# Sparse attention and a mixture of experts on one core: row maxima sent as columns by DMA, and tokens as the stationary operand in one block

## The chip, the cores and the metric

The kernel runs on one core of a Trainium2 chip. The metric is the device time of one execution in microseconds. The engines are named as the profile names them: PE (TensorE), with PEld for its weight loads, DVE (VectorE), ACT (ScalarE), POOL (GpSimd) and SP (SyncE). SPq and ACTq are the queues on which SP and ACT issue DMAs.

## The reference, cut to what matters

There are 8 batches of 8 heads with 576 rows and head width 64. Each row keeps only the scores that reach its 32nd largest one:

```python
scores = scale * np.matmul(q, k.transpose(0, 1, 3, 2))
kth = np.partition(scores, -top_k, axis=-1)[..., -top_k:-top_k + 1]
scores = np.where(scores >= kth, scores, -1000000000.0)
scores = scores - np.max(scores, axis=-1, keepdims=True)
attn = np.exp(scores); attn /= attn.sum(-1, keepdims=True) + 1e-09
x = np.matmul(attn, v)                       # then heads side by side: 4608 tokens x 512
do_compute = x @ w_skip > 0                  # the other tokens are passed on as they are
e_idx = np.argmax(xc @ w_gate, axis=1)       # xc: the tokens of do_compute; 8 experts
y[mask] = gate_w[mask, None] * (np.maximum(xc[mask] @ w1[e], 0.0) @ w2[e])
out[do_compute] = xc + y
```

The widths of an expert are 512, 1024 and 512.

## The kernel before, in words

**Attention** goes over 32 pairs of heads. q and k of a pair are loaded, turned on PE (L543), copied out by ACT (`put`, L548 and L554), split on POOL into a rounded high part and the rest (L568, L571), and brought by SP's DMAs (`copy`, L576) into the operands: `QH` and `KK` (128 partitions: high parts in one half, low parts of k in the other half) and `QL` (64 partitions: the low part of q, and below it two more rows). `KO` is the second operand's partner: the high part of k and, in the rows against those two rows of `QL`, the value -1. So what stands in the two rows of `QL` is subtracted from a query's scores in the same product. While the rows are searched they are zero.

A pair has nine **rows** (tiles of 128 queries by 576 keys; `row`). PE forms the scores in PSUM (`qk`, L659), DVE takes the eight largest of seven chunks (`chunk`, L669) and sorts among them (`cand`, L675 and L677), ACT copies the scores out (`take`, L711) and counts those above the 24th (`above_out`, L691, with a read of the accumulator), POOL sets those to zero (`push_out`, L714), DVE adds a marker and finds the next eight (`fill`, L723; `window`, L733), and ACT writes a penalty for everything below the 32nd (`below_out`, L730).

Then there are nine **units** to a pair (`unit`, `block`): PE forms the transposed scores (L873, with 128 partitions of `QH` and `KK`, and L875, with 66 partitions of `QL` and `KO`, which subtracts the maxima), adds the penalties (L880), and ACT takes the exponential (L905). `values` multiplies with v and forms sums and gate logits.

**The maxima** (`maxes`) are handed over twice in a pair, after rows 4 and 8. POOL rounds the column of five or four maxima into `NM` and puts what the rounding left out beside it (L821, L822), PE turns `NM` (L827), ACT copies the turned rows into `mt` (L831), and SP sends them to the two rows of `QL` by row DMAs (L837): four for the first head and two for the second.

**The order** within attention is made when the program is built. Each step goes to a planner (`Plan`) with an engine, a duration, a due time and the steps it follows; the planner sends the instruction that can start first, and among those that can, it takes the earliest due time. Due times are the row's number plus offsets from two tables of numbers, `K` and `FINE`. On each engine the instructions then run in the order in which they were sent. SP is in order too; a DMA that SP issues also waits for the DMA eight before it on SP's queue, since there are eight completion semaphores. There are three PSUM tiles for rows and units together.

**The experts** follow. Tokens are listed by expert in three blocks of 128 (`route`), gathered by POOL, turned (L1158), and multiplied with w1 (`up`, L1223 to L1225: w1 is stationary, the tokens move; three products for high and low parts) and with w2 (`down`, L1246 to L1248). The first expert's first two blocks are gathered before the last batch is done. Its third block waits for the last batch's routing, and is multiplied apart from the others, with 128 moving columns (`upping`). The weights of later experts are loaded and split two experts ahead (`part_hi` L1115 on ACT, `part_lo` L1118 on DVE).

## Time and profile before

| what | value |
|---|---|
| runs | 1150.28, 1151.07, 1150.89 us; median 1150.89 us |
| the profiled execution | 1151.41 us, its span 1149.4 us |
| busy, PE / DVE / ACT / POOL | 1103.8 / 985.4 / 929.3 / 764.9 us |
| instructions, PE / DVE / ACT / POOL | 13012 / 5226 / 1965 / 1027 |
| share of the DMA engines, queue 1 (SP) | 46.0% |

A busy time is the union of the instructions' spans on an engine. Neighbours on ACT and DVE overlap at their ends, so that a row of the timeline with a duration of 0.76 us can be followed 0.66 us after its start by the next; what an instruction costs is read from start to start of neighbours that wait for nothing.

In the stages: up to about 45 us the first rows fill the pipe, then attention runs evenly to about 830 us, its last pair ends at about 864 us, and from there the experts run to 1134 us; the last scattered rows go out behind that.

### The profile page before, as it was taken

To read this page: it belongs to the slowest core of one execution; us is meant where nothing else is said; L and a number is where in the kernel's file an instruction comes from. 1 tells how busy PE (TensorE), PEld (TensorE's weight loads), DVE (VectorE), ACT (ScalarE), POOL (GpSimd) and SP (SyncE) were. 2 spreads that over 40 slices of the span, in tenths; PEclk is the share of its full clock that TensorE was granted. 3 is DMA by queue.
4 is the path that set the end of the run, shared out by engine and by line. 5 is a ranking of instruction groups with operands and counts; after the bars stand their busy time and mean duration, and the time that the engine had idled before them with its cause. 6 is when DMAs were issued, how large, how long until landed. Compare 5 with 4: busy or idle time off the path is not lost. (4 is left out here: it accounts for less than half of the span.)

```text
span 1149.4 us, 37808 instructions
## 1 busy us (share of the span) xinstructions
PE 1103.8 (96%) x13012; PEld 939.4 (82%) x13012; DVE 985.4 (86%) x5226; ACT 929.3 (81%) x1965; POOL 764.9 (67%) x1027
## 2 busy tenths in 40 slices
PE   4799999999999999999999999999999999999996
PEld 4678888888888888888888878887778988899995
DVE  8899999999999999999999999999966756655541
ACT  4899999999999999999999999999972533444430
POOL 7777888888778888887788999888884121222211
PEclk9999999999999999999999999999999999999998
DMA  6544546565544555565446444654147554455300
GB/s 145 120 102 117 127 118 149 120 150 125 138 116 116 141 132 140 123 138 140 117 115 150 105 114 116 159 135 112 29 127 254 185 172 160 162 168 163 120 19 26
DMA packets 197405, 148.43 MB, mean 129 GB/s; under 512 B 100898, under 2 KB 162850, under 8 KB 197204
## 3 DMA queue, kind: packets, MB, share of 16 engines
q1 hardware_dynamic: 190340, 135.54, 46.0%
q0 software_dynamic: 3840, 9.47, 2.5%
q8 instruction: 105, 1.72, 0.6%
q10 hardware_dynamic: 3024, 0.90, 0.3%
q14 instruction: 96, 0.79, 0.2%
HBM read 68.31 MB, written 25.31 MB: 81 GB/s over the span
## 5 line engine op out<-in xcount | busy, mean ns | idle before, releaser
L714 POOL TENSOR_TENSOR xw<-xc,r 128x576 f32<-128x576 f32 x288 | 370.6, 1287 | 126.2 <-ACT r L691 120.4
L669 DVE MAX8 cand<-r 128x8 f32<-128x82 f32 (+1 forms) x2016 | 384.1, 234 | 3.6 <-PE r L659 1.1
L691 ACT ACTIVATE r<-xc,cl 128x576 bf16<-128x576 f32 x288 | 221.7, 770 | 5.5 <-DVE cl L675 4.4
L730 ACT ACTIVATE PEN<-xc,wn 128x576 bf16<-128x576 f32 x288 | 221.0, 769 | 5.0 <-DVE wn L733 4.8
L733 DVE MAX8 wn<-xw 128x8 f32<-128x585 f32 x288 | 217.1, 754 | 2.6 <-POOL xw L714 2.5
L873 PE MATMUL r<-QH,KK 128*128 128x256 f32 (+1 forms) x640 | 188.2, 321 | 5.0 <-ACT PT L905 2.1
L711 ACT ACTIVATE xc<-r 128x576 f32<-128x576 f32 x288 | 183.8, 639 | 6.0 <-DVE cand L669 2.9
L875 PE MATMUL r<-QL,KK 66*128 66x256 f32 (+1 forms) x640 | 173.3, 298 | 0.0
L659 PE MATMUL r<-KK,QH 128*128 128x288 f32 x640 | 161.5, 342 | 11.5 <-ACT xc L711 7.9
L675 DVE MAX8 cl<-cand 128x8 f32<-128x28 f32 (+2 forms) x864 | 164.5, 192 | 5.2
L905 ACT ACTIVATE PT<-r 128x576 f32<-128x576 f32 x256 | 161.8, 642 | 3.5 <-PE r L880 3.5
L1152 POOL DMA_INDIRECT out_dram<-ot,idx x24 | 24.0, 999 | 200.9 <-DVE ot L1151 155.3
L659 PE MATMUL r<-KK,QL 66*128 66x288 f32 x640 | 135.5, 302 | 0.0
L873 PEld LDWEIGHTS r<-QH,KK 128*128 128x128 f32 x640 | 118.3, 190 | 16.7 <-ACT xc L711 6.4
L880 PE MATMUL r<-nbi,PEN 128*128 128x128 bf16 (+1 forms) x1632 | 131.9, 216 | 0.0
L659 PEld LDWEIGHTS r<-KK,QH 128*128 128x128 f32 x640 | 98.0, 195 | 38.4 <-issue 12.1
L1115 ACT ACTIVATE hi<-raw 128x1024 fp32r<-128x1024 f32 x64 | 67.2, 1055 | 71.6 <-PE py L1248 71.3
L1118 DVE TENSOR_TENSOR lo<-raw,hi 128x1024 fp32r<-128x1024 f32 x60 | 73.3, 1225 | 59.1 <-ACT hi L1115 59.1
L875 PEld LDWEIGHTS r<-QL,KK 66*128 66x128 f32 x640 | 118.9, 191 | 0.0
L659 PEld LDWEIGHTS r<-KK,QL 66*128 66x128 f32 x640 | 104.3, 195 | 0.3 <-issue 0.3
L677 DVE MATCH_REPLACE8 cand<-cl,cand 128x28 f32<-128x28 f32 x576 | 103.0, 179 | 0.0
L880 PEld LDWEIGHTS <-PEN 128*128 128x128 bf16 x1632 | 82.3, 99 | 21.2 <-issue 0.4
(272 smaller groups left out, 2511.0 us busy)
## 6 DMA issues: line engine op xcount, KB each, us to landing
raw<-in_moe_w_dram SPq DMA_DIRECT2D x64, 512.0 KB
KK<-HI SPq DMA_DIRECT2D x62, 288.0 KB
QH<-HI SPq DMA_DIRECT2D x124, 144.0 KB
KK<-LO SPq DMA_DIRECT2D x62, 144.0 KB
QL<-LO SPq DMA_DIRECT2D x62, 144.0 KB
raw<-in_k_dram SPq DMA_DIRECT2D x64, 128.0 KB
V<-in_v_dram SPq DMA_DIRECT2D x32, 256.0 KB
raw<-in_q_dram SPq DMA_DIRECT2D x62, 128.0 KB
```

The lines of the kernel that those rows point to most:

```text
L659: nc.tensor.matmul(R(u, w), t[0:k0, c:c + P], KH[i2][0:k0, HB * hd + u:HB * hd + w], start=(k0 == P and x == 0), stop=(k0 < P and x == len ...
L669: nc.vector.max(C[s][:, c], R(CH[c], CH[c + 1]))
L675: nc.vector.max(L[:, 4 * r:4 * r + 8], c)
L691: nc.scalar.activation(RR[s], R() if i in SG else XC[s], AF.Sign, bias=CL[p][:, i, 23:24], scale=-ODD, accum_out=CN[:, s:s + 1])
L711: nc.scalar.activation(XC[s], R(), AF.Copy)
L714: nc.gpsimd.tensor_tensor(xw()[:, 0:S], XC[s], RR[s], op=OP.mult)
L730: nc.scalar.activation(pen, XC[s], AF.Relu, bias=least, scale=-1.0)
L733: nc.vector.max(WN[p][:, i], XW[s] if out_ else R())
L873: nc.tensor.matmul(t, KH[i2][:, ks], QH[i2][:, qs], start=(y == 0), stop=False)
L875: nc.tensor.matmul(t, KO[i2][:, ks], QL[i2][0:D + 2, qs], start=False, stop=False)
L880: nc.tensor.matmul(rb[:, O + c:O + c + z - a], PEN[p][:, PS * i + REM + c0 - o:PS * i + REM + c0 - o + P], nbi[:, a:z], start=False, stop= ...
L905: return pl.add("ACT", 0.535, due + K["ex"] + FINE["ex"][at], lambda: nc.scalar.activation(dst, st["r"], AF.Exp, scale=scale), x, give=[h])
```

## The change

**Maxima.** `NM` becomes two tiles of nine columns. POOL rounds the maxima into them with one copy, what the rounding left out is dropped, and SP sends each column of 128 maxima (64 for the halves of row 4) straight into its piece of `QL`'s single extra row, element by element: six DMAs for the first head and four for the second. PE's turning (L827), ACT's copy (L831) and POOL's second step (L822) are gone. `KO` and `QL` have 65 rows in use in place of 66.

**The first expert's third block** (`late`). The tokens are the stationary operand and w1's quarters move, with 256 columns to a product. The hidden values come out with the tokens on the partitions; two halves of 512 columns are copied to SBUF by ACT (`SL`), turned back on PE in two groups of four, and then go through the relu as before. The first half's `down` products are sent by the planner.

**The start.** The loads of the first q and k stand ahead of everything, on SP and ACT. The casts into `KK` on DVE write one half and are written as a maximum of the source with itself; the other half comes by two DMAs. The gate table's identities come by one DMA in place of twelve copies on POOL, and its clearing covers 18 columns of 146. Tables and clearings that are not needed first stand later. Unused branches are dropped.

**Offsets.** All of `K` and `FINE` is new, and with them the order on every engine. Some durations that the planner assumes are a little shorter (POOL's products 1.255 in place of 1.31).

```diff
-    nc.gpsimd.memset(NM_.bitcast(F32), 0.0)
+    NM_ = [ap_.tile([P, NR], F32R, name=f"NM{i}") for i in range(2)]
...
-            nc.gpsimd.tensor_copy(nm[:, 0:n], cl)
-            nc.gpsimd.tensor_tensor(nm[:, n:2 * n], cl, nm[:, 0:n], op=OP.subtract)
-            nc.tensor.transpose(pm[:, 0:P], NM_, identR)
-            nc.scalar.activation(mt, h.t[0:2 * n, 0:P], AF.Copy)
-            nc.sync.dma_start(dst[a:a + 1].bitcast(F32), src.bitcast(F32))
+        def send(j, r0, c):
+            n = P if j != NM else REM
+                nc.sync.dma_start(QL[p % NQ][D:D + 1, c:c + n].bitcast(F32), nm[r0:r0 + n, j:j + 1].bitcast(F32))
+        x = pl.add("POOL", 0.2, due + FINE["mx"][m0], lambda: nc.gpsimd.tensor_copy(nm[:, i0:i0 + n], CL[p][:, i0:i0 + n, 0]),
+                   [CAND0[NR * p + i] for i in range(i0, i0 + n)], MAXED.get((p - 2, i0 > 0)))
+        MAXED[p, i0 > 0] = [pl.add("SP", 0.67, due + 0.4, lambda y=y: send(*y), x, lag=2.0) for y in rows]
...
-                        nc.tensor.matmul(t, KO[i2][:, ks], QL[i2][0:D + 2, qs], start=False, stop=False)
+                        nc.tensor.matmul(t, KO[i2][:, ks], QL[i2][0:D + 1, qs], start=False, stop=False)
...
-    done = upping(EARLY * P, TN, D1 + 12, turning(0, NB - 1, PX, D1 + 8, g))
+        def product(i, ph):
+            for c in range(CC):
+                nc.tensor.matmul(o, xh[:, c], h1[:, c], start=(c == 0), stop=False)
+                nc.tensor.matmul(o, xh[:, c], l1[:, c], start=False, stop=False)
+                nc.tensor.matmul(o, xl[:, c], h1[:, c], start=False, stop=(c == CC - 1))
+        def back(g, px):
+            for k in range(FC // 2):
+                nc.tensor.transpose(px[:, k * P:(k + 1) * P], SL[g][:, k * P:(k + 1) * P], identF)
+    done = late(D1 + 12, turning(0, NB - 1, PX, D1 + 8, g))
...
-        ops = [("DVE", 0.7, KK[0][up, :, A], two(kA), None, 0), ("ACT", 0.55, QH[0][up, A], qA, None, 0),
+        ops = [("DVE", 0.7, KH[0][up, A], kA, None, 0), ("ACT", 0.55, QH[0][up, A], qA, None, 0),
...
-                    nc.vector.tensor_copy(dst, src)
+                    nc.vector.tensor_tensor(dst, src, src, op=OP.max)
...
-K = dict(qk=-6.898, cand=-10.286, kt=0.696, push=-15.422, ...)
+K = dict(qk=-3.229, cand=-70.654, kt=-66.095, push=-15.835, ...)
```

Where it moves instructions, three places. First SP's queue, over one handing-over of both heads' maxima in the middle of attention, before (L837 sends maxima, L576 brings operands, L509 and L510 load q and k; the numbers behind the names tell buffers apart):

```order
L837 DMA QL_115<-mt 1x4x128
L837 DMA QL_115<-mt 1x2x64
L837 DMA QL_115<-mt 1x4x128
L837 DMA QL_115<-mt 1x2x64
L576 DMA QL_112<-QL_112 2x1280
L509 DMA raw_117<-in_k_dram 128x4x64 x2
L510 DMA rawr<-in_k_dram 64x2x64
L509 DMA raw_118<-in_q_dram 128x4x64 x2
L510 DMA rawr<-in_q_dram 64x2x64
L837 DMA QL_115<-mt 1x4x128 x2
```

And now, from the first head's maxima on (L749 sends a column, L365 and L366 store results, L567 brings operands):

```order
L749 DMA QL_110<-NM_208 1x128x1 x4
L749 DMA QL_110<-NM_208 1x64x1 x2
L365 DMA xd<-xb 512x1x128
L366 DMA xd<-xb 64x128
L365 DMA out_dram<-xb 512x1x128
L366 DMA out_dram<-xb 64x128
L567 DMA KK_108<-HI 64x2x576
L567 DMA KK_108<-LO 64x576
L567 DMA QH_106<-HI 64x576 x2
L567 DMA QL_107<-LO 64x576
L567 DMA QL_107<-QL_107 1x16x80
```

Five more operand copies follow, and then the second head's four columns. What were six DMAs from `mt` are ten from `NM`; now the results' stores and eleven DMAs for the next operands stand between the two heads' maxima, where the loads stood before.

Next ACT's queue in the middle of attention, before:

```order
L730 ACTIVATE PEN_195<-xc,wn 128x576
L548 ACTIVATE TT<-pa 128x512
L905 ACTIVATE PT_123<-r_148 128x576
L831 ACTIVATE mt<-pt 10x128
L691 ACTIVATE r,CN<-xc,cl 128x576
L711 ACTIVATE xc<-r_147 128x576
```

And now, at about the same place (L695, L539, L812, L674 and L679 are the former L730, L548, L905, L691 and L711):

```order
L695 ACTIVATE PEN_203<-xc,wn 128x576
L812 ACTIVATE PT_130<-r_152 128x576
L674 ACTIVATE r,CN<-xc,cl 128x576
L679 ACTIVATE xc<-r_154 128x576
L887 ACTIVATE os_150<-pa 128x64
L885 ACTIVATE os_150<-pa 128x64
```

The row `mt` is gone from ACT; the others come as often as before, in another sequence.

Last PE's queue where the first expert's third block ends, now (L1181 to L1183 are the products, L1187 turns the hidden values back, L1058 turns the next expert's tokens, L1146 to L1148 are `down`):

```order
L1182 MATMUL ph<-lo_17551,xh_17554 128x256
L1183 MATMUL ph<-hi_17547,xl_17555 128x256
L1187 MATMUL px<-identF,sl_17910 128x128 x4
L1058 MATMUL px<-identF,xg_17887 128x128 x4
L1181 MATMUL ph<-hi_17548,xh_17554 128x256
```

Behind the fourth quarter's twelve products there are three `down` products, and then the second group of four turns. Before, eight groups of twelve products with 128 columns stood here, then all 24 `down` products of the block.

More of the change, by code (lines that the diff above doesn't have):

```diff
@@ L80, in tile_kernel, with load_raw @@
     ps_a = att.enter_context(tc.tile_pool(name="ps_a", bufs=1, space=PSUM))
+    RAW = [sp_.tile([P, NM, 2, D], F32, name=f"raw{i}") for i in range(2)]
+    RAWR = sp_.tile([P, 2, D], F32, name="rawr")
+    def load_raw(p, nm, queue):
+        b, hp = divmod(p, H // 2)
+        src = (k, q)[nm]
+        for hh in range(2):
+            queue.dma_start(RAW[nm][:, 0:NM, hh], src[b, 2 * hp + hh, 0:MAIN].rearrange("(p t) d -> p t d", p=P))
+        queue.dma_start(RAWR[nm * REM:(nm + 1) * REM], src[b, 2 * hp:2 * hp + 2, MAIN:S].rearrange("h p d -> p h d"))
+    load_raw(0, 0, nc.sync)
+    load_raw(0, 1, nc.scalar)
     identF = cp.tile([P, P], F32, name="identF")
@@ L276, in tile_kernel @@
     pl = Plan()
-    pl.at.update(ACT=3.0, DVE=6.0, POOL=12.0, SP=0.35)
+    pl.at.update(ACT=4.4, DVE=6.0, POOL=10.5, SP=0.35)
     BT = Res([lambda dt: ps_t.tile([P, 512], dt, name="pt"), lambda dt: ps_a.tile([P, 512], dt, name="pa")])
@@ L503, in load @@
     def load(p):
[L504 to L516 removed]
+        for nm in range(2):
+            if p:
+                LOADED[nm, p] = pl.add("SP", 2.0, max(NR * p - K["ld"], 0 if p == 1 else -99) + 0.5 * nm,
+                                       lambda nm=nm: load_raw(p, nm, nc.sync), TURNED.get((nm, p - 1)), lag=1.5)
+            else:
+                LOADED[nm, p] = pl.add("SP", 0.5, -99 + nm, None, lag=4.2)
     def load_v(p):
@@ L595, in prep @@
         if old:
-            COPIED[p].append(pl.add("SP", 0.67, NR * p - 3, lambda: copy(QL[i][D:D + 2], QL[i][D + 2:D + 4]), old, lag=2.0))
+            COPIED[p].append(pl.add("SP", 0.67, NR * p - 3, lambda: copy(QL[i][D:D + 1], QL[i][D + 1:D + 2]), old, lag=2.0))
     CFREE = {}
@@ L642, in row @@
         PEN[p] = PEN_[p % 2]
-        out_ = i in OUT
-        h = Hold(RW, 1 if out_ and i not in SG else 2)
+        h = Hold(RW, 1)
         R = lambda u=0, w=S: h.t[:, LO_ + u:LO_ + w]
@@ new lines, in row @@
+        rr = A("ACT", 0.765, s + D_["kt"] + J("kt"), above_out, x, tx, PUSHD.get(s - 3), lag=-0.06)
+        fx = A("DVE", 0.129, s + D_["push"] + J("fill"), fill, rr, OUTW[-2:-1])
+        PUSHD[s] = A("POOL", 1.255, s + D_["push"] + J("push"), push_out, rr, tx, OUTW[-2:-1])
+        wx = A("DVE", 0.675, s + D_["window"] + J("window"), window, PUSHD[s], fx, lag=0.09)
+        OUTW.append(wx)
+        WINS.setdefault(p, []).append(wx)
+        kx = PENNED[s] = A("ACT", 0.672, s + D_["rf"] + J("rf"), below_out, wx, TU.get(p - 2))
@@ L1082, in tile_kernel @@
     SUM, SUMMED, AVU, AVR, LASTSET, OSFREE, SETS, DONE = {}, {}, {}, {}, {}, {}, [0], {}
-    x = pl.add("POOL", 2.5, 5.0, clear_gate)
-    y = pl.add("SP", 5.0, 18.0, load_gate, x, lag=2.5)
-    x = [pl.add("POOL", 0.45, 6.0 + 0.5 * j, lambda j=j: turn_gate(j), x) for j in range(H + H // 2)]
-    GATE = x + [y, pl.add("DVE", 2.0, 8.0, tables)]
+    clear_gate()
+    GATE = [pl.add("SP", 0.65, 12.0, lambda x=x: load_gate(*x), lag=4.5) for x in gates]
     for p in range(NP):
@@ L1314, in checks @@
         rows = lambda a, u, w: a.rearrange("p (b i) -> p b i", i=NR)[:, :, u:w]
-        for u in sorted(set(OUT)):
+        for u in range(NR):
             cn, kt, ok = (rows(a, u, u + 1) for a in (CN, FL[:, 3], oks))
```

275 lines of the change are left out of this document (99 added, 176 removed).

## The prediction

> **What bounds the kernel now.** I read the page first. Its second part gives each engine's busy share in 40 slices of 28.7 us:
>
> ```profile
> PE   4799999999999999999999999999999999999996
> DVE  8899999999999999999999999999966756655541
> ACT  4899999999999999999999999999972533444430
> ```
>
> From the second slice to the 29th, PE, DVE and ACT are all above 90%; from there on PE alone is. So there are a start, an even stage of attention, and the experts, and each has its own limit. The table by stretches (length, then busy time and instructions of PE, PEld, DVE, ACT and POOL) gives the even stage and one stretch that is worse:
>
> ```profile
> 300.00:400.00 100.00, 99.71 (x1411) 83.40 (x1400) 98.43 (x601) 99.25 (x221) 80.05 (x102) 1.00 0.53 130
> 600.00:700.00 100.00, 97.31 (x1355) 81.35 (x1353) 97.36 (x582) 96.20 (x210) 90.24 (x128) 1.00 0.49 117
> ```
>
> Three engines at 98 to 100% can't all be the limit, so I looked for hidden waits. First ACT's timeline (start, duration) where nothing is waited for:
>
> ```profile
> 299.84 0.25 ACT L831 ACTIVATE mt<-pt 8x128 fp32r<-8x128 f32 x1
> 300.00 0.62 ACT L905 ACTIVATE PT<-r 128x576 f32<-128x576 f32 x1
> ```
>
> Start to start, ACT goes from one instruction to the next without a gap, and copying the turned maxima costs it 0.16 us (299.84 to 300.00). Then DVE's timeline, the same operation at two places:
>
> ```profile
> 299.91 0.17 DVE L675 MAX8 cl<-cand 128x8 f32<-128x28 f32 x1
> 300.00 0.23 DVE L669 MAX8 cand<-r 128x8 f32<-128x83 f32 x1
> ...
> 301.84 0.19 DVE L675 MAX8 cl<-cand 128x8 f32<-128x28 f32 x1
> 302.07 0.09 DVE L677 MATCH_VALUE_LOAD cand<-cl,cand 128x8 f32 x1
> ```
>
> The sort step takes 0.09 us where the next instruction doesn't need it and 0.23 us where it does: DVE's busy time holds waits on itself, which other chunks could fill. ACT has none of that kind. Its waits over 40 to 830 us (us in total, times, longest) are short; the two largest are:
>
> ```profile
> ACT r L691 <- DVE cl L675: 3.6, 8, 0.7
> ACT xc L711 <- DVE cand L669: 1.8, 10, 0.3
> ```
>
> So ACT's instruction stream is what attention waits for, with PE close behind. From 100 to 600 us the count below gives 177 rows in 500 us, which is 2.82 us a row and 25.4 us a pair of nine:
>
> ```profile
> L691 ACT ACTIVATE r<-xc,cl 128x576 bf16<-128x576 f32 x177 | 136.0, 768 | 0.3
> ```
>
> **The change, part by part: maxima.** These groups of the whole execution go away on ACT:
>
> ```profile
> L831 ACT ACTIVATE mt<-pa 10x128 fp32r<-10x128 f32 (+1 forms) x34 | 8.6, 254 | 0.0
> L831 ACT ACTIVATE mt<-pt 8x128 fp32r<-8x128 f32 (+1 forms) x30 | 7.6, 254 | 0.9 <-DMA QL<-mt 0.9
> ```
>
> That is 64 instructions at 0.16 us from start to start, 10.2 us of the engine that sets the pace (16.2 us by their spans, which overlap their neighbours). PE loses 64 turns, POOL 64 small subtractions; they only make room for the same gain. A pair would take 25.4 - 0.32 = 25.1 us. Not all of it will come: the first pairs' copies lie in the start, and DVE, whose work is the same, has to fill more of its own waits. From below, if DVE's 98.43 of 100 us were all work, 1.57 us per 100 could go at best, and a quarter of it is a cautious end: 3 us over some 800. From above it is 10.2 us. I take 8.5 us, nearer the upper end, since the two rows of L675 show that DVE's busy time isn't all work. The new offsets add an uncertainty of their own: the stretch from 600 to 700 us lost 3.0 us more of ACT than the one from 300 to 400 us, and one such stretch more or less is worth 3 us either way.
>
> SP pays for this. Its queue in a later pair, and the small loads of the gate, which move 4 bytes to a piece:
>
> ```profile
> 415.92 2.72 SPq L837 DMA_DIRECT2D QL<-mt  x4
> 422.95 0.58 SPq L576 DMA_DIRECT2D QL<-QL  x1
> ...
> 33.79 0.63 SPq L306 DMA_DIRECT2D G<-in_moe_w_skip_dram  x1
> 34.47 0.61 SPq L305 DMA_DIRECT2D G<-in_moe_w_skip_dram  x1
> ```
>
> An issue takes 0.68 us, and small pieces make it no slower (33.79 to 34.47). A pair has 30 DMAs on SP now (six loads of q and k, three of v, eleven for operands, six of maxima, four stores) and will have 34. That is 4 x 0.68 = 2.7 us more, and the queue stood still for 4.3 us in this pair (415.92 + 2.72 = 418.64 to 422.95). So I cost it at nothing; the cover is that gap, and 34 x 0.68 = 23.1 us a pair must stay under 25.1 us. Behind the columns are queued stores and operands of the next pair, for which PE's rows wait. What the pieces cost the DMA engines is in the queue's line (packets, MB, share of 16 engines) from 34 to 36 us, when hardly anything else moved:
>
> ```profile
> q1 hardware_dynamic: 1118, 0.01, 29.8%
> ```
>
> 1118 packets took 0.298 x 16 x 2 = 9.5 us of engine time, 8.5 ns each. A pair's 1152 elements make 9.8 us on 16 engines, 0.6 us of the queue's transfer time in 25 us, with the engines at 0.53. The landing of such a column the trace doesn't show. By the Trainium skill's "DMA: Bandwidth & Descriptors" (Bandwidth), transfers under 64 KB are dominated by their descriptors, which speaks against columns of 512 bytes; if each held the queue for the fixed 2.0 us that its anatomy section gives, ten of them would add about 13 us to each pair's queue (an estimate from that page), and the time would rise by hundreds of us. The rows at 33.79 and 34.47, 0.68 us apart, show that the queue goes on without waiting.
>
> **The third block.** PE's timeline of products with 128 and 256 columns, of four turns, and the place where PE waited for the block's tokens:
>
> ```profile
> 855.71 0.28 PE L873 MATMUL r<-QH,KK 128*128 128x256 f32 x1
> 855.83 0.28 PE L875 MATMUL r<-QL,KK 66*128 66x256 f32 x1
> ...
> 887.63 0.63 PE L1158 MATMUL px<-identF,xg 128*128 128x128 f32 x4 [0.66 <-DMA xg<-xd,idx]
> ...
> 890.80 0.27 PE L1223 MATMUL ph<-xh,hi 128*128 128x128 f32 x1
> 890.91 0.27 PE L1224 MATMUL ph<-xl,hi 128*128 128x128 f32 x1
> ...
> 891.47 0.62 PE L1158 MATMUL px<-identF,xg 128*128 128x128 f32 x4
> 891.85 0.31 PE L1223 MATMUL ph<-xh,hi 128*128 128x128 f32 x1
> ```
>
> A product with 128 columns costs 0.11 us and one with 256 costs 0.12, so twice the columns are nearly free. Before: 96 x 0.112 = 10.8 us (0.11 and a little more at the turns). After: 48 x 0.12 = 5.8 us, and two groups of four turns at 0.38 us, 0.8 us: together 6.5 us. The saving is 4.2 us, and PE is the limit here:
>
> ```profile
> 900.00:920.00 20.00, 20.00 (x123) 19.04 (x122) 14.65 (x20) 11.48 (x17) 3.34 (x4) 1.00 0.76 241
> ```
>
> The new way out (ACT's copy, the turns, the relu) is hidden for the first half by the fourth quarter (1.4 us) and for the second by one trio of down products, which may leave PE idle for up to 0.5 us twice. The next expert's weights come free earlier with the products. When the block starts is set by the routing and the gather (the wait of 0.66 us), which the change doesn't shorten. I take 4 us, between 2.5 and 4.4.
>
> **The start.** From the timeline of the first 18 us:
>
> ```profile
> 5.29 0.57 ACTq L509 DMA_DIRECT2D raw<-in_q_dram  x1
> 10.57 2.70 DVE L621 CAST KK<-TT 64x1152 fp32r<-64x1152 f32 x1 [2.13 <-ACT TT L554]
> 11.08 1.57 POOL L293 MEMSET G<- 128x1752 f32 x1
> 13.30 0.75 DVE L617 TENSOR_TENSOR KK<-TT,KK 64x576 fp32r<-64x576 f32 x1
> 14.20 0.82 PE L659 MATMUL r<-KK,QH 128*128 128x288 f32 x2 [3.23 <-DVE KK L617]
> 15.36 0.76 DVE L621 CAST KK<-TT 64x1152 fp32r<-64x1152 f32 x1
> ```
>
> q's second load was issued at 5.29 us, behind ACT's first work, and now stands first. DVE's first cast took 2.70 us beside POOL's clearing of the gate table, and the same cast 0.76 us later on; the new form, half as long with two inputs, has its row in L617, 0.75 us. That is 2 us off the chain to the first product at 14.20. What q's earlier load could give beyond that is mostly lost, as I read the new order: DVE has its tables and clearings ahead of the first cast still, and POOL's counting for them stands behind three more clearings. I take 2 us, between -1 (a loss) and 4. The Trainium skill's "GPSIMD Engine Reference" (Specifications) names two SBUF inputs, too, as a cause of contention with VectorE: by that the new form would stall as the cast did, and the sum would be 2 us higher. The two-input row at 13.30 kept its 0.75 us, but POOL's long clearing was over by then, so the trace leaves this open.
>
> **The sum.** 1151.4 (the profiled execution) - 8.5 - 4 - 2 = 1136.9 us. The runs' median lies 0.5 us under that execution, which gives 1136.4; I say 1136.5 us. Less than 0.2%, 2.3 us, can't be told from no change.
>
> **The rivals.** *DVE takes over.* With ACT relieved, DVE's chains (sort, window, next row) become what ends last, and the even stage gives 1 to 3 us. For it: DVE at 98.43 and an unchanged amount of work on it; against it: the waits inside. It gives 1150.9 - 2 - 4 - 2 = 1143 us, between 1141 and 1146. Chance 0.2.
>
> *Nothing arrives.* The new order costs on ACT what the removed copies give, by two or three more stretches like 600 to 700 us, and part of the late block's gain goes into waits of the new chain. Some 10 us of 14.5 are eaten and the start gives nothing: 1147 to 1150 us. For it: every place in the order has changed. Against it: only one stretch of the old order is bad. Chance 0.1, half of it within 0.2% of before.
>
> *SP becomes the bound (slower).* 34 issues fit a pair of 25.1 us as long as one takes less than 0.74 us with its waits. For the maxima alone it is 0.68; a DMA that must wait for the eighth before it, or for data behind which others queue, takes more. At 0.76 us a pair needs 25.8 us in place of 25.4, which is 0.44 x 31 = 13.6 us more; with 6 us from the start and the late block, 1158.5 us. Against it: the gap of 4.3 us and 8.5 ns an element. Chance 0.1.
>
> **The numbers.** The forecast has 0.6, and by itself it ranges from 1132 (all three upper ends, 10.2 + 4.4 + 4 = 18.6 us) to 1141 (5 us less in the even stage). The range of 1130 to 1148 takes in DVE's case, part of the third, and below 1132 the bad stretch going away; outside are SP's case and the rest, under 0.2. Faster: 0.6 + 0.2 + 0.05 = 0.85. Within 0.2%: 0.05. Slower: 0.1.
>
> **What would show it.** In the profile of the changed kernel, 100 us of the even stage should hold 35.8 rows in place of 35.4, with ACT still above 99 and DVE near 99 of 100; the third block's products should take 6.5 us on PE from its first to its last turn, less the next expert's turns; the first product should start at about 12 us. The forecast is wrong if ACT's share falls to 97 and DVE or PE waits take its place, if rows or units wait for DMAs of `QL`, or if SP's queue shows no gap in a pair.

## The result and the profile after

The changed kernel takes 1164.73 us (median of five runs, 1162.47 to 1165.33), the kernel before 1150.89 us (1150.28 to 1151.07): a ratio of 1.0116, 95% interval 1.0101 to 1.013. It is slower by 13.8 us where 14.4 us faster was forecast, and outside the range. The profiled execution took 1162.81 us, its span is 1160.7 us, 11.3 us more than before.

The busy shares in 40 slices, with the granted clock of TensorE as the last row, from the page of the changed kernel:

```profile
PE   4799999999999999999999999999998999999996
DVE  7899999999999999989999999999865656655541
ACT  5899999999999999999999999999872533444420
PEclk9599999999999999999999999999998999999998
```

In attention they look much as before, but for one eight on DVE in the middle. The granted clock is lower in the second slice and, with PE at eight, in the 31st, where the experts begin. The table by stretches says more; here is the changed kernel's (length, then busy time and instructions of PE, PEld, DVE, ACT and POOL, granted clock, DMA share, GB/s):

```profile
300.00:400.00 100.00, 98.37 (x1407) 83.11 (x1406) 98.69 (x603) 99.52 (x214) 79.36 (x96) 1.00 0.59 130
...
500.00:600.00 100.00, 94.49 (x1302) 79.93 (x1300) 93.69 (x571) 94.79 (x203) 74.42 (x88) 0.97 0.59 125
600.00:700.00 100.00, 97.42 (x1360) 82.37 (x1358) 98.32 (x593) 98.92 (x210) 78.47 (x97) 1.00 0.60 132
```

From 300 to 400 us ACT runs seven instructions fewer than before (214 for 221) and is no less busy (99.52 for 99.25). From 500 to 600 us PE, DVE and ACT are each some 5% less busy than in the kernel before, which had:

```profile
500.00:600.00 100.00, 99.50 (x1418) 82.86 (x1417) 98.88 (x608) 99.30 (x222) 81.67 (x106) 1.00 0.55 134
```

PE's waits from 100 to 830 us (us in total, times, longest) show what for; in the changed kernel:

```profile
PE r L783 <- ACT PT L812: 6.3, 31, 0.6
PE pt L534 <- DMA rawr<-in_q_dram: 5.1, 5, 2.3
PE pa L534 <- DMA rawr<-in_q_dram: 2.9, 3, 1.6
```

and in the kernel before the largest was:

```profile
PE pa L993 <- ACT os L982: 1.3, 4, 0.4
```

PE now waits for the load of q, eight times. The load is issued on SP, so here is SP's queue ahead of the longest of these waits, and then the wait on PE:

```profile
508.92 2.26 SPq L567 DMA_DIRECT2D QH<-HI  x2
511.23 0.60 SPq L567 DMA_DIRECT2D QL<-LO  x1
511.93 2.49 SPq L749 DMA_DIRECT2D QL<-NM  x4
514.52 1.27 SPq L81 DMA_DIRECT2D raw<-in_q_dram  x2
515.83 0.63 SPq L82 DMA_DIRECT2D rawr<-in_q_dram  x1
516.56 0.54 SPq L513 DMA_DIRECT2D V<-in_v_dram  x1
517.20 1.69 SPq L516 DMA_DIRECT2D VR<-in_v_dram  x2
518.94 0.62 SPq L365 DMA_DIRECT2D xd<-gt  x1
```

```profile
519.58 0.45 PE L534 MATMUL pt<-identF,rawr 128*128 128x128 f32 x1 [2.33 <-DMA rawr<-in_q_dram]
```

Each row starts within 0.1 us of the end of the one before: the queue has no gap, the columns (L749) stand ahead of the load, and the load's last part goes out at 515.83, 3.75 us before PE can use it. In the kernel before, the same load of a pair in the even stage went out some 18 us ahead of its use:

```profile
123.43 0.66 SPq L510 DMA_DIRECT2D rawr<-in_q_dram  x1
141.17 0.27 PE L543 MATMUL pa<-identF,rawr 128*128 128x128 f32 x1
```

Where the 11.3 us lie is read from the first and last of the 288 row steps (count, then ns, then first and last start), before and after:

```profile
L691 ACT ACTIVATE r<-xc,cl x288: 755/762/849, 20.4 to 844.6; 128x576 bf16<-128x576 f32 x144
```

```profile
L674 ACT ACTIVATE r<-xc,cl x288: 759/781/925, 21.1 to 852.2; 128x576 bf16<-128x576 f32 x144
```

and from the last score block and the experts' first product, here the changed kernel's:

```profile
L812 ACT ACTIVATE PT<-r x256: 626/666/787, 44.5 to 864.4; 128x576 f32<-128x576 f32 x128
```

```profile
L1123 PE MATMUL ph<-xh,hi x256: 270/323/535, 877.5 to 1133.0; 128*128 128x352 f32 x112, 128*128 128x224 f32 x16
```

Before, these were at 856.5 and 864.8 us. So attention is 7.9 us later at its last block (0.7 of it from the first row on), the handover takes 13.1 us for 8.3, 4.8 more, and from the first product to the end of the span it is 283.2 us for 284.5, 1.3 less. Together 11.3 or 11.4 us. The even stage was forecast at 35.8 rows per 100 us for 35.4 before, counted from 100 to 600 us. Over that stretch the changed kernel has 174 rows for 177, which is 34.8 per 100 us; only from 200 to 400 us does it keep the old pace (71 rows for 70).

### The profile page after: what moved, and what is told of

Its sections match the earlier page's. It is cut to its first block, busy times and chain, and to the rows that moved or that the text cites. A ratio compares the mean times of both kernels' runs of the same rounds, so it can differ in the third digit from the quotient of the medians.

```text
span 1160.7 us, 37398 instructions
## 1 busy us (share of the span) xinstructions
PE 1098.5 (95%) x12908; PEld 939.1 (81%) x12908; DVE 978.9 (84%) x5226; ACT 926.9 (80%) x1902; POOL 747.0 (64%) x949
## 4 chain that ended last, share of the span: by engine, by line
DVE 36%; PE 34%; ACT 15%; issue 6%; POOL 4%; DMA 3%; SPq 1%; POOLq 0%; ACTq 0%; DVEq 0%
DVE cand L660 13%; DVE wn L698 8%; ACT r L674 5%; DVE cand L668 5%; DVE cl L666 5%; PE py L1146 4%; PE py L1148 4%; PE py L1147 4%; PE ph L1123 4%; PE ph L1124 4%; PE ph L1125 3%; ACT xc L679 3%; ACT PEN L695 3%; PE r L651 3%; POOL xw L682 2%
## 5 line engine op out<-in xcount | busy, mean ns | idle before, releaser
L660 DVE MAX8 cand<-r 128x8 f32<-128x82 f32 (+1 forms) x2016 | 380.8, 234 | 13.8 <-PE r L651 12.8
L674 ACT ACTIVATE r<-xc,cl 128x576 bf16<-128x576 f32 x288 | 226.9, 788 | 9.1 <-DVE cl L666 8.3
L695 ACT ACTIVATE PEN<-xc,wn 128x576 bf16<-128x576 f32 x288 | 226.9, 790 | 8.7 <-DVE wn L698 7.1
L783 PE MATMUL r<-QH,KK 128*128 128x256 f32 (+1 forms) x640 | 192.6, 328 | 12.9 <-ACT PT L812 6.3
L679 ACT ACTIVATE xc<-r 128x576 f32<-128x576 f32 x288 | 189.1, 658 | 4.8 <-DVE cand L660 2.9
L785 PE MATMUL r<-QL,KK 65*128 65x256 f32 (+1 forms) x640 | 174.1, 299 | 0.0
L812 ACT ACTIVATE PT<-r 128x576 f32<-128x576 f32 x256 | 166.4, 665 | 3.6 <-PE r L790 3.5
L651 PE MATMUL r<-KK,QH 128*128 128x288 f32 x640 | 161.4, 342 | 6.0 <-ACT xc L679 5.8
L1052 POOL DMA_INDIRECT out_dram<-ot,idx x24 | 25.3, 1052 | 198.8 <-DVE ot L1051 153.6
L651 PE MATMUL r<-KK,QL 65*128 65x288 f32 x640 | 135.5, 302 | 0.0
L785 PEld LDWEIGHTS r<-QL,KK 65*128 65x128 f32 x640 | 119.7, 193 | 0.0
L651 PEld LDWEIGHTS r<-KK,QH 128*128 128x128 f32 x640 | 99.0, 197 | 23.6 <-issue 8.4
L651 PEld LDWEIGHTS r<-KK,QL 65*128 65x128 f32 x640 | 104.8, 196 | 0.0
```

Of the source, the lines that this page charges most:

```text
L651: nc.tensor.matmul(R(u, w), t[0:k0, c:c + P], KH[i2][0:k0, HB * hd + u:HB * hd + w], start=(k0 == P and x == 0), stop=(k0 < P and x == len ...
L660: nc.vector.max(C[s][:, c], R(CH[c], CH[c + 1]))
L674: nc.scalar.activation(RR[s], XC[s], AF.Sign, bias=CL[p][:, i, 23:24], scale=-ODD, accum_out=CN[:, s:s + 1])
L679: nc.scalar.activation(XC[s], R(), AF.Copy)
L695: nc.scalar.activation(pen, XC[s], AF.Relu, bias=least, scale=-1.0)
L783: nc.tensor.matmul(t, KH[i2][:, ks], QH[i2][:, qs], start=(y == 0), stop=False)
```

## The experiments

Each is compared with the kernel before on the same chip; its medians there lie between 1150.5 and 1151.4 us, so a difference between two of the runs below is good to about 1 us. Theory Q says that SP's queue is the bound: with ten columns a pair it has 34 DMAs to issue, and all slack is gone. The rival says that the new offsets order the work badly.

**Three loads a pair moved to GpSimd's queue** (on the changed kernel):

```
-            nc.sync.dma_start(V[p % 4]...            # and VR, twice
+            (nc.gpsimd if p > 3 else nc.sync).dma_start(V[p % 4]...
...
```

> The changed kernel, its plan and order unchanged, but the three loads of V of each pair (from the fifth pair on) are issued from GpSimd's queue and no longer from SP's: 31 issues a pair on SP for 34. Output unchanged. Theory Q (SP's queue is the bound): in the changed kernel SP issued 267 DMAs between 200 and 400 us, 0.749 us apart, with 1.2 us of gaps in all; 34 x 0.749 = 25.5 us a pair is the pace of the pairs, and the load of q comes 3 us ahead of its transposes. With 31 issues SP needs 23.2 us a pair: gaps of about 2 us a pair come back, PE's waits for the load of q go, and the 6 us lost between 480 and 540 us return: 1154 to 1159. Rival O (the new offsets order the work badly): SP is not what it waits for, 1162 to 1166 as the changed kernel. A third case: GpSimd pays for the issues with about 1 us each, the products of scores and rows wait behind them, and the time is above 1166.

Measured: 1201.63 us, ratio 1.0428 (1.0405 to 1.045). It is the third case. SP's gaps did come back (24.1 us between 200 and 400 us), but GpSimd pays; its timeline in one pair:

```profile
320.38 1.28 POOL L682 TENSOR_TENSOR xw<-xc,r 128x576 f32<-128x576 f32 x1 [0.19 <-ACT r L674]
321.63 1.57 POOL L562 TENSOR_TENSOR LO<-TT,HI 128x640 fp32r<-128x640 f32 x1
323.13 0.77 POOL L513 DMA_DIRECT2D V<-in_v_dram  x1
323.89 1.04 POOL L516 DMA_DIRECT2D VR<-in_v_dram  x2
324.95 1.31 POOL L682 TENSOR_TENSOR xw<-xc,r 128x576 f32<-128x576 f32 x1
```

The products of rows (`xw`), one of which each row needs every 2.8 us, are 4.6 us apart here: 1.8 us of issues stand between them, besides a split (`LO`). DVE's longest entry in its list of waits (100 to 830 us) is for these products; the changed kernel's list has no such entry:

```profile
DVE wn L698 <- POOL xw L682: 24.1, 44, 1.2
```

PE's waits for the load of q, which Q said would go, did not: they grew from 8.0 us in eight waits to 14.8 us in nine, and SP now had to wait for GpSimd's rounded maxima (12.3 us between 200 and 400 us). So the run can't tell Q from its rival.

**Six of ten columns left out** (on the changed kernel, same plan):

```
         def send(j, r0, c):
+            if p and j % KC in (1, 2, 3) and j != NM:
+                return
```

> The changed kernel, its plan and order unchanged, with six of the ten column DMAs of each pair left out (the maxima of six row tiles do not reach the second operand, but for the first pair): 28 issues a pair on SP for 34. Theory Q: 28 x 0.749 = 21.0 us a pair, SP has 4 us of gaps a pair as the kernel before, PE's waits for the load of q go: 1153 to 1159, near the run with V on GpSimd's queue without the price that GpSimd may pay there. Rival O: 1162 to 1166. If the columns cost nothing but their issue, nothing else moves; should it fall below 1150, the column DMAs cost more than their issue.

Measured: 1152.72 us, ratio 1.0011 (1.0002 to 1.0021). 12.0 us of the 13.8 are back, just beyond the range that Q gave. SP has 37.1 us of gaps between 200 and 400 us, PE's waits for the load of q are gone from its list, and the bad stretch is healed (500 to 600 us, same columns as above):

```profile
500.00:600.00 100.00, 98.57 (x1405) 82.98 (x1404) 98.44 (x606) 99.45 (x215) 78.56 (x96) 1.00 0.61 136
```

What stays is the first entry of the changed kernel's list, PE waiting for the exponentials (6.3 us there), so that one is not SP's:

```profile
PE r L785 <- ACT PT L814: 6.2, 30, 0.6
```

**Six more issues a pair in the kernel before:**

```
             nc.sync.dma_start(dst[a:a + 1].bitcast(F32), src.bitcast(F32))
+            nc.sync.dma_start(XTRA[n:n + 1], ones[0:1, 0:8])     # n counts up
```

> The kernel before with one more DMA of 32 bytes issued on SP right behind each of its six row DMAs of maxima: 36 issues a pair for 30. Nothing reads what they write; output, plan and order unchanged. The kernel before issued 236 DMAs between 200 and 400 us with 27.3 us of gaps, so 0.732 us each. Theory Q: 36 x 0.732 = 26.4 us a pair against the 25.35 us of its pace: SP becomes the bound, 1.0 us a pair over some 28 pairs, 1170 to 1185. Rival O: SP's load does not matter at this size, 1150 to 1153.

Measured: 1158.57 us, ratio 1.0071 (1.0055 to 1.0088). The sign is Q's, the size is less than half of what was expected. Two rows of SP's queue show one reason, the price of what was added:

```profile
515.51 0.67 SPq L838 DMA_DIRECT2D QL<-mt  x1
516.23 0.40 SPq L841 DMA_DIRECT2D xtra<-ones  x1
```

A DMA of 32 bytes takes 0.40 us to issue. With 281 issues and 1.2 us of gaps in 200 us the queue is full, at 0.707 us an issue. The loss is 7.4 us by the last row; 4.3 of it come from the 168th row to the 192nd, where eight stores of gates (`xd<-gt`, from 503 to 525 us) are issued besides. That these stores cause it was not tested.

**The old offsets in the changed kernel** (the two tables of numbers, nothing else):

> The changed kernel with the two tables of offsets of the kernel before; all else of the change stays: 34 issues a pair on SP. Theory Q: SP is still the bound at 25.5 us a pair, whatever the order: 1158 to 1175 (the offsets were not made for this work, so more waits than in the changed kernel can come). Rival O: the offsets are what lost the time; with the old ones the terms of the prediction come out, 1136 to 1148.

Measured: 1166.45 us, ratio 1.0124 (1.0093 to 1.0156). With SP at 34 issues the two sets of offsets can't be told apart (the intervals overlap); the rival, that the new ones alone lost the time, falls.

**Two columns left out**, `if p and j in (1, 6): return`:

> The changed kernel, plan and order unchanged, with two of the ten column DMAs of each pair left out (the maxima of two row tiles do not reach the second operand, but for the first pair): 32 issues a pair on SP, for 34 (1164.73 us) and 28 (1152.72 us). Theory Q says where the limit lies: 32 x 0.745 = 23.8 us a pair is below the pace of 25.3, with about 1.5 us of gaps, so most of the 12 us that six columns gave back come back with two: 1152.5 to 1156. Rival: the column DMAs cost by the element or by their landing, so that each column left out gives back its sixth of 12 us: 1159.5 to 1162.

Measured: 1156.02 us, ratio 1.0046 (1.003 to 1.0062), at the upper edge of Q's range: two columns give back 8.7 us of the 12.0 that six give. So the cost is not the same for each column: most of it lies between 32 and 34 issues, and 3.3 us between 28 and 32.

**Nine more in the kernel before** (two behind each DMA of the rounded maxima, one behind each of the rest):

> The kernel before with nine more DMAs of 32 bytes a pair on SP, two behind each row DMA of the rounded maxima and one behind each of the remainders: 39 issues a pair for 30 (1150.89 us) and 36 (1158.57 us, at 0.71 us an issue and no gaps). Nothing reads what they write; output, plan and order unchanged. Theory Q: 39 x 0.71 = 27.7 us a pair against 25.35: 2.3 us over some 28 pairs, 1205 to 1225. Rival: the seven microseconds of the run with six more were stray waits, one for each DMA, and nine cost half as much again: 1160 to 1164.

Measured: 1175.65 us, ratio 1.0211 (1.018 to 1.0242): neither range. Nine cost 25.1 us where six cost 7.1, each against the kernel before on its own chip, so it is a limit that is passed and not a price each. The expectation had counted 0.71 us for each added one; at 0.40 us the limit is passed by less. PE's longest entry in the list of waits is now a row of maxima that SP sends late:

```profile
PE r L879 <- DMA QL<-mt: 13.2, 16, 2.3
```

SP's queue between 200 and 400 us, counted from its timeline in nine runs (of each gap, what exceeds 0.15 us is counted; the price of an issue is 200 us less the gaps, divided by the issues):

| kernel | issues a pair | issues | gaps, us | price, us | time, us |
|---|---|---|---|---|---|
| before | 30 | 236 | 27.3 | 0.732 | 1150.89 |
| changed | 34 | 267 | 1.2 | 0.745 | 1164.73 |
| two columns out | 32 | 252 | 10.0 | 0.754 | 1156.02 |
| six columns out | 28 | 219 | 37.1 | 0.744 | 1152.72 |
| changed, old offsets | 34 | 267 | 2.7 | 0.739 | 1166.45 |
| turned row (below) | 27 | 208 | 46.8 | 0.737 | 1171.56 |
| V on GpSimd | 31 | 235 | 24.1 | 0.748 | 1201.63 |
| before, six more | 36 | 281 | 1.2 | 0.707 | 1158.57 |
| before, nine more | 39 | 293 | 3.7 | 0.670 | 1175.65 |

But for the two runs with 32-byte DMAs, the price is nearly the same whether the queue is full or a fifth of it is idle. It is a mean that holds short waits: in the changed kernel 218 of the 267 issues are followed by the next within 0.8 us, after 0.66 us in the mean, and the other 49 take longer, while SP's own list names 45 waits for other engines in that time. 34 x 0.745 = 25.3 us is the pace of a pair itself, with nothing to spare.

So an even pair is no slower than before, and the time goes where something comes on top. Against the run with six columns out, which has the same order, the changed kernel's rows are late by 1.4 us at the 165th row (486 us), 3.2 at the 174th (514 us) and 7.8 at the 178th (530 us), of 9.9 at the last. Between 500 and 560 us it issues eight stores of gates besides, 8 x 0.745 = 6.0 us of the queue. They are not the whole reason: the first of PE's long waits for q there, 1.58 us, ends at 491.56, ahead of the first of these stores at 501.74. And behind the second, which ends at 519.58, TensorE's granted clock was at half until 525.66; 2.8 of the 7.8 us come there, from the 176th row to the 178th, and what of them is the clock was not tested.

**The third block alone**, on the kernel before:

```
-    done = upping(EARLY * P, TN, D1 + 12, turning(0, NB - 1, PX, D1 + 8, g))
+    done = late(D1 + 12, turning(0, NB - 1, PX, D1 + 8, g))       # late() as in the change
...
-                    down(f, j, PY[j])
+                    if e or f >= FC // 2:
+                        down(f, j, PY[j])
```

> The kernel before with one part of the change alone: the first expert's third block has its tokens as weights. Output unchanged. In the profile of the changed kernel the experts took 272.5 us from the first 224-column product to the last product of the last expert, for 273.6 before, though about 30 products at their start ran at 213 ns apart for 111 ns at half the granted clock, 3 us. Theory: the part is worth the 4 us that the prediction gave it, 1145.5 to 1148.5. Rival: the ACT copies, the turns back and the waits for them eat what the shorter products save, as the 1.0 us in the changed kernel's profile says, 1149 to 1151.

Measured: 1147.73 us, ratio 0.9972 (0.9961 to 0.9983): 3.3 us, in the theory's range. The gain lies where it was forecast: from the experts' first product to the last it is 270.1 us for 273.6. This is the fastest kernel of the study that does all the work, and beats both the kernel before and the changed one. The block's products on PE, first and last, with its own turns between:

```profile
889.06 0.28 PE L1281 MATMUL ph<-hi,xh 128*128 128x256 f32 x1
889.17 0.28 PE L1282 MATMUL ph<-lo,xh 128*128 128x256 f32 x1
...
895.89 0.28 PE L1283 MATMUL ph<-hi,xl 128*128 128x256 f32 x1
...
897.39 0.63 PE L1287 MATMUL px<-identF,sl 128*128 128x128 f32 x4 [0.19 <-DVE hl L1301]
```

**The rounded row by TensorE, ACT and a row DMA, with the old offsets:**

```
+            nc.tensor.transpose(h(F32R)[:, 0:P], NM_, identR)
...
+            nc.scalar.activation(st["mt"], h.t[0:n, 0:P], AF.Copy)
...
-                nc.sync.dma_start(QL[p % NQ][D:D + 1, c:c + n].bitcast(F32), nm[r0:r0 + n, j:j + 1].bitcast(F32))
+            nc.sync.dma_start(dst.bitcast(F32), st["mt"][u:w].bitcast(F32))      # three a pair
```

> The changed kernel with two things back: the offsets of the kernel before, and the maxima's way through TensorE, ACT and one row DMA; but of the rounded maxima alone, so that a pair has 3 such DMAs where the kernel before had 6 and the changed kernel 10 columns, and SP 27 issues a pair. The 64 ACT copies are there again. Output unchanged. Against the run with the old offsets (1166.45 us) it differs by the columns alone. Theory Q (34 issues a pair bind SP): with 27 SP has 5 us of gaps a pair, no wait for the load of q, and the third block and the start are kept: 1143 to 1150. Rival: it is not SP but the old offsets with this start and these transposes that lose the time, 1158 to 1168.

Measured: 1171.56 us, ratio 1.0178 (1.0164 to 1.0192): Q's number fails, and the rival's range is passed as well. SP is idle for nearly a quarter of the time, and yet a pair of the even stage takes 26.3 us for 25.3 in the changed kernel. ACT's longest entry in its list of waits (100 to 830 us) is

```profile
ACT r L674 <- DVE cl L666: 10.7, 25, 1.2
```

ACT waits for the sort on DVE; why that is late was not looked into. So Q explains the changed kernel, but with SP relieved something else, most likely the order, can cost more than SP does.

**The old offsets with six columns left out:** the edits of those two runs together.

> The changed kernel with the offsets of the kernel before and six of the ten column DMAs of each pair left out (the maxima of six row tiles do not reach the second operand, but for the first pair): 28 issues a pair on SP. Theory Q: SP's limit hid the offsets; without it the terms that were measured alone add up under the old offsets, 4.3 us of ACT copies and 3.3 us of the third block from 1150.9: 1142 to 1148. Rival O: the old offsets do not fit the changed work, and cost here what they cost in the run with the turned row (1171.56 us at 27 issues): 1155 to 1168.

Measured: 1160.42 us, ratio 1.0082 (1.0068 to 1.0096): the rival. With SP relieved, the new offsets (1152.72) are 7.7 us better for this work than the old; under SP's limit that could not be seen (1164.73 and 1166.45). The terms measured alone did not add up here.

**ACT's copies left out of the kernel before**, and **done twice**:

```
-            nc.scalar.activation(mt, h.t[0:2 * n, 0:P], AF.Copy)      # left out: MT, a constant, is sent
...
+            nc.scalar.activation(mu, h.t[0:2 * n, 0:P], AF.Copy)      # twice: behind the first
```

> The kernel before without the 64 ACT copies of the turned maxima and nothing else: order and all other instructions stay, the row DMAs send zeros from a constant tile (so the scores' exponents go without their maxima, and these DMAs no longer wait for ACT). 64 x 0.16 = 10.2 us less on ACT. Theory A (the prediction's: ACT sets the pace of attention): 8.5 us less, 1141 to 1144. Theory B (ACT and VectorE stand so close that VectorE takes over; the changed kernel with six columns out ran at 25.31 us a pair for 25.41): 0.1 us over 30 pairs, 1146.5 to 1150.

> The kernel before with each of its 64 ACT copies of the turned maxima done a second time into a tile that nothing reads, and nothing else: 10.2 us more on ACT; output and order unchanged. Theories A and B say the same here, since ACT is then the longest: 7 to 11 us more, 1158 to 1162. Under 1154 ACT would have real slack and not be among the bounds at all.

Measured: 1146.64 us, ratio 0.9965 (0.9952 to 0.9979), and 1157.47 us, ratio 1.0058 (1.0045 to 1.0072). Without them 4.3 us of 10.2 come out, the better end of theory B's range; twice costs 6.6, just under the range. ACT's share between 200 and 400 us tells none of this; without the copies, in the kernel before, and with them twice (the fourth pair of numbers is ACT's):

```profile
200.00:400.00 200.00, 199.45 (x2815) 167.38 (x2818) 197.41 (x1209) 198.34 (x426) 160.87 (x206) 1.00 0.54 131
```

```profile
200.00:400.00 200.00, 199.46 (x2783) 167.03 (x2780) 197.12 (x1198) 198.59 (x441) 160.10 (x205) 1.00 0.53 130
```

```profile
200.00:400.00 200.00, 198.67 (x2774) 165.70 (x2765) 196.12 (x1186) 198.66 (x451) 158.53 (x202) 1.00 0.53 130
```

ACT is at 99.2 to 99.3% in all three, and PE is at 99.3% or more, DVE at 98.1 to 98.7%. So the runs show that ACT does not bound attention alone, but not whether VectorE, as theory B has it, or PE is next. What differs is the length of the same instruction; without the copies, and with them twice (least, median, longest ns):

```profile
L691 ACT ACTIVATE r<-xc,cl x288: 758/792/894, 20.5 to 839.2; 128x576 bf16<-128x576 f32 x144
```

```profile
L691 ACT ACTIVATE r<-xc,cl x288: 755/760/830, 20.4 to 851.1; 128x576 bf16<-128x576 f32 x144
```

**The start's order** (on the run with six columns out):

```
-                                       lambda nm=nm: load_raw(p, nm, nc.sync), TURNED.get((nm, p - 1)), lag=1.5)
+                                       lambda nm=nm: load_raw(p, nm, nc.sync), TURNED.get((nm, p - 1)), lag=1.5 if p > 1 else 6.0)
```

> The run with six columns left out (1152.72 us), with one number of the plan changed: the second pair's load is counted as landing 6.0 us after its issue for 1.5, so that the second pair's first transposes no longer stand ahead of the first products of rows on PE; leaves out what that run left out. There PE waited 4.7 us for the second pair's k, and the first products came at 14.3 us though their operands were there at about 12. Theory S: with the order turned the first products come at 12.0 to 12.6 us, the first row's second step at 19 for 21.1, and the 2 us that the prediction gave to the start appear at the end: 1150 to 1151.5. Rival: the first rows wait for DVE and ACT behind that anyway and the start gives nothing that is still there at row 36: 1152 to 1154.

In the changed kernel the first products of rows (L651) come behind a turn of the second pair that waits for its load:

```profile
13.54 1.08 PE L534 MATMUL pa<-identF,raw 128*128 128x128 f32 x4 [4.72 <-DMA raw<-in_k_dram]
14.28 0.83 PE L651 MATMUL r<-KK,QH 128*128 128x288 f32 x2
```

With the other order they come at 11.75:

```profile
11.75 0.82 PE L651 MATMUL r<-KK,QH 128*128 128x288 f32 x2 [3.42 <-DVE KK L607]
```

Measured: 1152.54 us, ratio 1.0017 (1.0008 to 1.0027), the same as without the edit. The first row step is at 18.2 us for 21.1, but the 25th is 1.2 us later, and from there to the 40th all are some 1 us later: the rival.

**The handover: the routing's spacing, the lists on VectorE, the wait filled.** The changed kernel's first gather on POOL, its landing on PE and the products behind it:

```profile
867.71 1.29 POOL L1045 DMA_INDIRECT xg<-xd,idx  x1 [1.44 <-issue]
```

```profile
874.66 1.11 PE L1058 MATMUL pt<-identF,xg 128*128 128x128 f32 x4 [4.19 <-DMA xg<-xd,idx]
...
877.47 0.54 PE L1123 MATMUL ph<-xh,hi 128*128 128x224 f32 x1
878.67 0.55 PE L1124 MATMUL ph<-xl,hi 128*128 128x224 f32 x1 [0.67 <-DVE xl L1066]
```

Three runs were about it. The first has one offset of before, `rs=1.526` for 2.41; the second changes `if late and end` to `if late and b0 + nb >= B - 1` for the engine of the lists' compares; the third, on the changed kernel, adds to the first turning

```
+        for _ in range(36 if (e, j) == (0, 0) else 0):
+            nc.tensor.matmul(px[:, 0:P], onesb, onesb, start=True, stop=True)
```

> The run with six columns left out (1152.72 us), with one offset of the kernel before, that of the spacing of the routing's steps: on GpSimd's queue the last lists before the first gather then stand some ten row tiles earlier, and the gather is no longer behind 15 of their compares. Leaves out what that run left out. Theory H (the handover: the gather is late because GpSimd's lists are): PE's wait of 4 us for the gathered tokens goes, and with it the half clock of the 10 us behind it that cost 3 us: 1145 to 1149. Rival: the gather waits for the last stores or for the end of attention, and moving the lists changes nothing: 1151 to 1154.

> The run with six columns left out (1152.72 us), with three of five compares of the lists of the last batches but one on VectorE instead of GpSimd; leaves out what that run left out. Theory H: between the last score block and the first experts' product lie 12.9 us there, for 8.3 in the kernel before, because 15 compares of 0.6 us and two more operations stand ahead of the first gather on GpSimd, and PE waits 4.0 us for the gathered tokens and then runs 10 us at half clock. With 9 compares fewer the gather is 4 us earlier: 1145 to 1149. Rival: the gather is held by something else (the stores of the last tokens), 1151.5 to 1154.

> The changed kernel with 36 products of 128x128 bf16 of a constant on TensorE, into the tile that it writes next, right ahead of the first transposes of gathered tokens, where it waits 4.2 us for them. Output unchanged; nothing else is added. Theory C (TensorE loses half its clock because it idles, and the 10.2 us at half clock behind the wait cost 3 us, as 30 products at 213 ns for 111 ns say): the granted clock stays 1.0 there and the time is 1160.5 to 1163, against 1164.73 of the changed kernel. Rival: the clock falls there for another reason, or what follows waits for other engines anyway: 1164 to 1166.

Measured: 1159.66 us (ratio 1.0074, 1.0058 to 1.0089), 1157.54 us (1.0069, 1.0051 to 1.0087) and 1160.68 us (1159.59 to 1165.6; ratio 1.0098, 1.008 to 1.0115). The first two miss both ranges: the gather of the second was 9.4 us earlier than with six columns out (848.4 for 857.8 us), but the last row step came 5.3 us later and the last score block 9.8. Two things stood ahead of the last rows: DVE did nine compares between 832.7 and 840.0 us, and right behind them, at 840.57, ended a wait of 2.83 us of ACT for DVE's chunks; and on GpSimd the clearing ahead of the gather waited 3.92 us for PE. How much each cost was not tested. The third lies in theory C's range, though not by C's reason. It kept the clock, as its stretch from 872 to 886 us shows beside the changed kernel's (0.63):

```profile
872.00:886.00 14.00, 10.77 (x88) 9.71 (x89) 11.44 (x26) 6.66 (x13) 8.46 (x20) 1.00 0.59 175
```

but from the first product to the last it took 272.9 us, for 272.5 in the changed kernel: PE waited 1.62 us for DVE and 1.30 us for the next gather instead. Most of what its profile gains (1.5 of 2.0 us) lies before the last row. So filling the wait made the experts no shorter.

## Why the prediction was wrong

**SP "at nothing" is the step that failed.** It said: an issue takes 0.68 us, 34 of them 23.1 us, under 25.1. The 0.68 came from a stretch with four plain row DMAs and no wait. As the price of a plain issue it holds; as the mean of a pair it does not. Over 200 us of the same profile the queue issued 236 DMAs with 27.3 us of gaps, 0.732 us each, and 34 x 0.732 = 24.9 us would have left 0.2 us a pair, not 2. The gap of 4.3 us that it named as the cover occurs in every second pair (four times from 200 to 400 us); the mean gap is 3.5 us a pair, and four more issues take 2.9 of it. What was left went where more is issued or waited for than in an even pair, above all from 486 to 530 us. So one of the prediction's own signs of being wrong came true: SP's queue has 1.2 us of gaps in 200 us. What it named as late first was not what came first: rows and units waiting for `QL` did not show in the changed kernel; the load of q, which stands behind the columns, was late. A fixed 2.0 us for each column, which it had set aside, did not come: four took 2.49 us (511.93). Six columns out and the runs with added DMAs show the cause, two columns out where most of the cost begins.

The rival *SP becomes the bound* had the bound and its threshold (0.74 us an issue; measured 0.745), at a chance of 0.1. How it came to 1158.5 us is not what happened. It had each of 31 pairs 0.44 us slower at 0.76 us an issue; at the measured 0.745 the same sum gives 25.3 us a pair and no loss against 25.4, and the loss lies in a few places. That its 13.6 us for SP are near the 12.0 measured is luck.

**The maxima's term was mis-sized.** 8.5 us was taken of bounds 3 to 10.2; the copies alone are worth 4.3 us. ACT does set the pace when it has more to do (twice the copies, 6.6 us), but with less another engine is next at once. The rival *DVE takes over* was right that only part would come; that it is DVE and not PE, which is at 99.7% without the copies, no run shows. The reason for going to the upper end, that DVE's busy time holds waits, was not strong enough. With six columns out, where SP is not in the way, attention is 3.0 us shorter from the first row step to the last.

**The third block was right:** 4 us forecast between 2.5 and 4.4, 3.3 us measured alone. 6.5 us were forecast for its products and own turns; from 889.06 to 896.01 us are 6.95 us, in which two turns of the next expert take 0.7 and one of the two own ones is not yet done (0.4): 6.6 us. In the changed kernel only 1.0 us of it is seen between the first and the last product. That stretch began at half clock, but with the clock kept it was no shorter (272.9 for 272.5 us), so where the rest went is open.

**The start was right in DVE's chain and wrong in its worth.** The operands are there at about 12 us, as forecast, but PE's order puts a turn ahead that waits for a load; that row of the order was not read. What the prediction left open is settled: the two-input form took 0.71 us (L611, at 10.12 us) while GpSimd cleared a tile from 9.86 to 11.02, and 0.75 us (L607, at 11.65) beside another clearing, so it did not stall as the cast had. With the order mended, the first product is at 11.75 us and nothing of it is left from the 25th row on. The term is 0 for -2; with the turn in front, the changed kernel is some 0.9 us behind around the 35th row (0.1 to 2.3 us from row to row).

**The new offsets were under-priced at 3 us either way.** With SP out of the way they are worth 7.7 us against the old ones for this work. In the handover they cost part of the 4.8 us: from the last score block to the experts' first product it takes 13.1 us (12.9 with six columns out), with the old offsets 10.2 us (10.0), and 8.3 in the kernel before. The gather stands behind 15 compares on GpSimd, but bringing it forward in two ways made the last pair longer by as much or more. What order would give both is open, and so is the whole cause of those 4.8 us.

In the terms of the sum: -4.3 (copies), -3.3 (third block), 0 (start) are 7.6 us of gain, 1143.3 us without SP and the order. SP takes 12.0. The rest up to 1164.7 us, 9.4 us, is a remainder that no run shows as one thing. The order is the likely place, since every place in it has changed; but the terms were measured one by one on the kernel before and need not add up on the changed one. Of the 9.4 us only the handover's 4.8 and the start's 0.9 are seen by themselves.

## What to carry to other kernels

Before a queue is costed at nothing, take its price as the stretch less the gaps, divided by all issues in it, and hold the sum against the pace of the stage with its fullest repetition, not the usual one; here 0.05 us on an issue was most of the cover that had been counted on. An engine at 99% is not shown to be the bound by that share: look at whether the same instruction is at its shortest, or take its work away. And read the order of the engine that waits at the place of each gain, since a gain in one chain ends at the next in-order instruction that waits for another.

## What was not expected of the hardware

ACT's busy time hardly moves when its instructions in 200 us go from 441 to 426 or 451 (198.59, 198.34, 198.66 us), while the kernel's time goes from 1150.9 to 1146.6 or 1157.5 us. The median of the same 128x576 instruction goes from 762 ns to 792 and 760 instead: the slack hides in the spans. The Trainium skill's "Perfetto Trace Analysis" (Identifying the Most-Contended Engine) uses occupancy to find the bottleneck and calls it, for this engine, also a fair measure of how close one is to roofline; here the share stayed at 99% and showed neither the slack nor the lack of it.

A DMA issued on SP costs 0.73 to 0.75 us of its queue in the mean, short waits included, whether the queue is full or a fifth of it is idle, and 0.40 us if it moves 32 bytes to one place. The same page of the Trainium skill (DMA Optimizations) says that balancing DMAs over the engines that can issue may help when their generation is the limit. Here three a pair on GpSimd cost 37 us more than on SP; in the pair shown 1.8 us of issues stood ahead of work that rows wait for.

TensorE's granted clock fell to half in stretches that are multiples of 3.41 us (27.31 us from 27 us on, 6.83 from 519 us, 10.24 from 874 us in the changed kernel), the last two right at waits of 2.33 and 4.19 us; with the second of these filled by products the clock stayed. The Trainium skill's "TensorE: Matmul & The Clock Gate" (Part 1) gives a window of 3413 ns after which an idle array is slowed. The lengths agree; that the array is idle for the whole window does not show here, since in the 3.41 us ahead of the drop at 518.83 PE was busy for 1.83 us. What the half clock cost is not settled: the run with the mended start had full clock from 27 us on and the same time, the filled handover waited elsewhere, and behind the drop at 518.83 the rows lost 2.8 us.
